# First loads in another order, and the queries' block diagonals loaded by their non-zero quarters

## The chip, the cores and the metric

The kernel runs on one core of a Trainium2 chip. A core has five engines that follow their own instruction streams and meet at semaphores: TensorE (PE; its weight load is PEld), VectorE (DVE), ScalarE (ACT), GpSimd (POOL) and SyncE (SP), which here issues all DMAs. Sixteen DMA engines move the data between the memory of the chip (HBM) and the core's own. The metric is the device time of one execution in microseconds (us); the profile is of another execution, taken by the hardware profiler.

## The reference

Inputs are q, k and v of 2 batches, 8 heads, 768 positions and 64 values per head. Each query attends to the positions less than 16 away, and to 24 summaries, one for each block of 32 positions. Two feed-forward layers follow.

```python
k_sum = k.reshape(B, H, nb, block, D).max(axis=3)
v_sum = v.reshape(B, H, nb, block, D).mean(axis=3)
scores_l = where(abs(i - j) < 16, scale * q @ k.T, -1e9)
scores_s = scale * q @ k_sum.T + log(32)
a = softmax(concatenate([scores_l, scores_s]))
x = a @ concatenate([v, v_sum])             # 1536 tokens x 512
h = x @ w_in                                # 512 x 1024, float64 weights
h = h * softmax(h); h = layer_norm(h) * g_ln
x = h @ w_out                               # 1024 x 512
out = elu(x @ w_in2) @ w_out2               # 512 x 2048, 2048 x 512
```

## The kernel before

**Attention.** The 1536 tokens are cut into 24 tiles of 64 queries (n = 0 to 23, twelve of each batch). For tile n, `attn_s(n)` multiplies the queries with a window of 96 keys and the 24 block maxima (four matmuls of 128x128 by 128x120, two heads each; 120 = 96 + 24), adds a mask and makes the softmax on VectorE, ScalarE and GpSimd. `attn_p(n)` transposes the result on TensorE, and `attn_x(j)` multiplies tiles 2j and 2j+1 with their values and splits the product into a high and a low part, `xT[j]`. To hold two heads in one matmul, the queries come as block diagonals: `qd[n]` is 128 partitions x 4 head pairs x 128, where partitions 0 to 63 have values in the first 64 columns of each pair alone, and partitions 64 to 127 in the last 64. The host writes the zeros. `load_q(n)` (L192) loads this block whole, 256 KB in rows of 2 KB, into one of four rotating buffers `q_bd`.

`load_k(b)` loads the keys of batch b in four DMAs of 400 KB, `sum_k(b)` takes the block maxima on VectorE. `sum_v(b)` (L181) loads the values of batch b in six DMAs of 256 KB and makes the block means with six products on TensorE (twelve matmul records), which use the constant `avg`. `load_v(n)` loads the 96 values' rows of tile n (192 KB) into one of four buffers `vws`. From tile 12 on `load_kw(n)` loads the window of keys of a tile (192 KB, as 512 pieces of 384 bytes); before, GpSimd copies it from the keys.

**Weights.** `w_in` is float64. It comes in eight pieces of 512 KB (n = 0, 1 and k = 0 to 3), each into one of six places `early`, and is converted by ScalarE, GpSimd and VectorE into two float32 parts (`convert`, L141). Before the change `load_w_in` (L154) issues the load and the conversion together, and `more()` (L443) takes the next of the eight. `w_out` follows in eight pieces (`load_w_out`, one in each of the ticks 2 to 9).

**Order.** After a warm-up of 32 matmuls on a tile of zeros (L463 to L467) comes a first part written out by hand (L471 to L499), then a loop over 24 ticks (L515). In tick t the attention runs ahead: `attn_s(t + 6)`, `attn_x` of tiles up to t + 3, `attn_p(t + 4)`, beside `mm_in(j, n)`, twelve matmuls of the first feed-forward layer. Tick 0 holds `sum_v(1)`, tick 1 begins with `load_k(1)`. Without a load in the text before it, `attn_s(n)` loads its own queries. The SP queue is in manual order: SP issues the DMAs as the program names them, and when one has to wait, those behind it wait too. The other engines' orders come from a planner that simulates a timeline. `v_sb` and the keys share two buffers (tag "k"), so that `load_k(1)` must wait until the products of `sum_v(1)` have read theirs.

Of the kernel before, what the change touches and what calls it, by code (L numbers as in the profile page):

```python
# [22 lines left out]
TQ = 64  # L23
# [14 lines left out]
NKW = 4  # L38
NV = 4
NCOPY = 12  # L40
NG = 4


# [10 lines left out]
def tile_kernel(ctx: ExitStack, tc: tile.TileContext, qd, kT, v, w_in, w_out, g_ln, w_in2, w_out2,  # L54
# [39 lines left out]
    kws = [p_at.tile([128, NP, KW], F32, name=f"kw{i}", bufs=1) for i in range(NKW)]  # L94
    vws = [p_at.tile([128, DM], F32, name=f"vw{i}", bufs=1) for i in range(NV)]
    avg = p_at.tile([128, 128 + NB], F32, name="avg", bufs=1)
    nc.gpsimd.memset(negh, -0.5)
    nc.gpsimd.memset(guard, 1e-12)

# [16 lines left out]
    def load_words(bits, src):  # L116
        nc.sync.dma_start(bits, src if len(src.shape) == 3 else src.rearrange("p (k f) -> p k f", k=KD))
# [33 lines left out]

    early = stage[0] + stage[1] + stage[2]

    def load_w_in(n, k):  # L154
        cs = slice(n * 512, (n + 1) * 512)
        convert(early[(n * KD + k) % 6], w_in[k * 128:(k + 1) * 128, cs].bitcast(I32),
                w_in_hl[0][:, k, cs], w_in_hl[1][:, k, cs])

    def load_w_out(k):
        load_words(early[k % 6], w_out[k * 128:(k + 1) * 128, :].bitcast(I32))  # L160
# [7 lines left out]
    def load_k(b):  # L168
        k_sb[b] = p_k.tile([128, NP, S + 2 * PAD], F32, tag="k", name="k_sb", bufs=2)
        for p in range(NP):  # L170
            nc.sync.dma_start(k_sb[b][:, p, :], kT[b, p])
# [7 lines left out]


    def sum_v(b):  # L181
        pst = psb.tile([128, DM], F32, tag="b", name="vs_ps")
        v_sb = p_k.tile([128, NP, S + 2 * PAD], F32, tag="k", name="v_sb", bufs=2).rearrange("p a s -> p (a s)")
        for i in range(S // 128):
            vt = v_sb[:, i * DM:(i + 1) * DM]
            nc.sync.dma_start(vt, v[b, PAD + i * 128:PAD + (i + 1) * 128, :])
            c0 = NB - i * 4
            nc.tensor.matmul(pst, lhsT=avg[:, c0:c0 + 128], rhs=vt, start=i == 0, stop=i == S // 128 - 1)
        vsum[b] = p_at.tile([128, DM], F32, tag="vsum", name="vsum", bufs=1)
        nc.scalar.activation(vsum[b][WIN:KW, :], pst[WIN:KW, :], AF.Copy)  # L190

    def load_q(n):  # L192
        q_bd[n] = p_at.tile([128, NP, 2 * TQ], F32, tag="q", name="q_bd", bufs=4)
        nc.sync.dma_start(q_bd[n], qd[n])

    def load_v(n):
        b, t = divmod(n, NT)
        nc.sync.dma_start(vws[n % NV][0:WIN, :], v[b, t * TQ:t * TQ + WIN, :])
# [237 lines left out]
        yf["B22"] = form("y1", b22)  # L436


    conv = [lambda n=n, k=k: load_w_in(n, k) for n in range(2) for k in range(KD)]
    words = [lambda k=k: load_w_out(k) for k in range(KF1)]  # L440
    parts = [lambda k=k: convert_w_out(k) for k in range(KF1)]

    def more(n=1):  # L443
        for _ in range(n):
            if conv:
                conv.pop(0)()

    def mm_in(j, n):
        for k in range(KD):
# [18 lines left out]

    loads = tc.manual_schedule(engines={mybir.EngineType.SP})
    loads.__enter__()  # L470
    load_k(0)  # L471
    load_q(1)
    load_v(0)
    nc.sync.dma_start(mask, mask_d)
    sum_k(0)
    nc.sync.dma_start(ident, ident_d)
    load_q(0)
    more()
    nc.sync.dma_start(avg, avg_d)
    attn_s(0)  # L480
    more()
    attn_s(1)
    sum_v(0)
    more(2)
    attn_p(0)
    attn_p(1)
    attn_s(2)
    load_v(1)
    attn_x(0)
    nc.sync.dma_start(gT, g_ln)  # L490
    attn_s(3)
    load_v(2)
    attn_p(2)
    attn_s(5)
    more(3)
    attn_p(3)
    attn_s(4)
    load_v(3)
    more()  # L499

# [12 lines left out]
    for t, (j, n) in enumerate(ticks):  # L515
        s_n, p_n, x_n = t + LEAD, t + LEAD - 2, t + LEAD - 3
        if t == 0:
            sum_v(1)
        elif t == 1:
            load_k(1)  # L520
        elif t == 3:
            sum_k(1)
        if t % 2:
            for u in (x_n, x_n + 1):
                if u < NU:
                    load_v(u)
        if s_n < NU:
            for u in (s_n + 1, s_n):
                if u < NU and u not in q_bd:
                    load_q(u)  # L530
            load_kw(s_n + 1)
            attn_s(s_n)
        if x_n < NU and x_n % 2:
            attn_x(x_n // 2)
        mm_in(j, n)
        if p_n < NU:
            attn_p(p_n)
        for f, *args in after[t]:
            f(*args)
        for _ in range(fetches.get(t, 0)):  # L540
            words.pop(0)()
        for _ in range(converts.get(t, 0)):
            parts.pop(0)()
        if t == min(late) - 1:
            fetch()
        if t == 14:
            spare[:] = stage[2]
        more_w(late.get(t, 0))
        if x_n == NU - 1:
            p_at.release()  # L550
            p_w3 = ctx.enter_context(tc.tile_pool(name="p_w3", bufs=1, side="left", reuse_waits="tile"))
            for f in (3, 4):
                w3t[f] = p_w3.tile([128, 2048], F32, tag=f"f{f}", name="w3f")
            w3e[0] = p_w3.tile([128, 2, 3, 2, 128], F32R, name="w3e")
            last_t = p_w3.tile([128, 2, KF1, TB], F32R, tag="last", name="lnT")
            lnT_last = [last_t[:, c] for c in range(2)]
# [229 lines left out]
```

## Time and profile before

| what | us |
|---|---|
| median of 3 runs (lowest to highest) | 479.52 (479.25 to 479.68) |
| profiled execution, its own time | 480.95 |
| its span, first to last instruction | 479.2 |
| TensorE busy | 464.0 |
| VectorE, ScalarE, GpSimd busy | 298.6, 286.9, 122.3 |
| DMA queue of the kernel, as a share of 16 engines | 52.1% |

The profiled execution lies 1.4 us above the median, and 1.75 us of it lie outside the span. Busy time of TensorE is the union of modelled instruction times: it holds the warm-up's matmuls too, and a busy stretch can hold small holes. Times in the rows count from the start of the span.

### The profile page before, as it was taken

How to read it: one execution, taken by the hardware profiler on the slowest of the kernel's cores; microseconds unless marked ns; L12 is line 12 of the kernel's file. 1: busy time of each engine (PE TensorE's matmuls, PEld its weight loads, DVE VectorE, ACT ScalarE, POOL GpSimd, SP SyncE). 2: the span in 40 equal slices, each digit the busy share in tenths (PEclk: the TensorE clock that was granted, in tenths of full speed). 3: DMA queues.
4: the chain of work that ended last, by engine and by line, in shares of the span. 5: the costliest groups of instructions: out<-in, count | busy, mean ns of one | idle time of the engine just before them, and what ended most of it. 6: DMA issues, size and time to landing. Idle time of an engine off the chain costs nothing.

```text
span 479.2 us, 7413 instructions
## 1 busy us (share of the span) xinstructions
PE 464.0 (97%) x2600; PEld 390.1 (81%) x2600; DVE 298.6 (62%) x664; ACT 286.9 (60%) x647; POOL 122.3 (26%) x213
## 2 busy tenths in 40 slices
PE   7789999899999999999999999999999999999996
PEld 3456788789988989999888888888888888888885
DVE  3786779885568529786998893367665565450000
ACT  1795697986568428475957673567667666560001
POOL 2795276755443512332222200000000000000000
PEclk9999999999999999999999999999999999999999
DMA  8996995462280543388879614442212222377112
GB/s 284 353 365 185 297 299 174 127 193 77 84 256 19 166 133 130 118 291 315 244 273 385 213 54 136 172 175 60 72 51 83 88 60 73 133 297 274 44 44 88
DMA packets 40116, 82.46 MB, mean 172 GB/s; under 512 B 9616, under 2 KB 18448, under 8 KB 40080
## 3 DMA queue, kind: packets, MB, share of 16 engines
q1 hardware_dynamic: 40080, 82.00, 52.1%
q8 instruction: 20, 0.33, 0.3%
q14 instruction: 16, 0.13, 0.1%
HBM read 70.46 MB, written 11.53 MB: 171 GB/s over the span
## 4 chain that ended last, share of the span: by engine, by line
PE 86%; DMA 8%; DVE 3%; ACT 1%; SPq 1%; issue 0%
PE o_ps L110 9%; PE o_ps L108 9%; PE o_ps L109 9%; PE h L110 7%; PE h L108 7%; PE h L109 7%; PE c L110 5%; PE c L108 5%; PE c L109 5%; DMA q_bd<-in_qd 5%; PE y_ps L108 5%; PE y_ps L110 5%; PE y_ps L109 5%; PE s_ps L218 3%; PE t_ps L299 2%; DMA vw<-in_v 2%
## 5 line engine op out<-in xcount | busy, mean ns | idle before, releaser
L129 POOL TENSOR_SCALAR conv<-conv 128x512 f32<-128x512 f32 x48 | 37.6, 785 | 81.2 <-ACT conv L126 79.6
L232 POOL TENSOR_SCALAR sm<-sm,st 128x120 f32<-128x120 f32 x96 | 43.8, 472 | 30.7 <-DVE st L230 14.3
L108 PE MATMUL o_ps<-w4r,g_hl 128*128 128x512 f32 x128 | 49.8, 389 | 0.0
L109 PE MATMUL o_ps<-w4r,g_hl 128*128 128x512 f32 x128 | 49.8, 389 | 0.0
L110 PE MATMUL o_ps<-w4r,g_hl 128*128 128x512 f32 x128 | 46.7, 389 | 0.0
L108 PE MATMUL y_ps<-lnT,w_out 128*128 128x384 f32 x128 | 43.6, 341 | 0.8 <-ACT y L316 0.8
L227 ACT ACTIVATE sm<-sm,st 128x120 f32<-128x120 f32 x96 | 37.0, 390 | 10.7 <-DVE st L224 10.7
L109 PE MATMUL y_ps<-lnT,w_out 128*128 128x384 f32 x128 | 43.2, 337 | 0.0
L110 PE MATMUL y_ps<-lnT,w_out 128*128 128x384 f32 x128 | 42.9, 336 | 0.0
L108 PE MATMUL h<-w_in,xT 128*128 128x512 f32 x96 | 39.3, 411 | 0.8 <-ACT xT L138 0.8
L110 PE MATMUL h<-w_in,xT 128*128 128x512 f32 x96 | 38.5, 401 | 0.8 <-DVE xT L105 0.8
L109 PE MATMUL h<-w_in,xT 128*128 128x512 f32 x96 | 38.4, 400 | 0.0
L224 DVE CUSTOM_DVE_ANT_0 sm<-s_ps,mask 128x120 f32<-128x120 f32 x96 | 21.6, 277 | 14.6 <-PE s_ps L218 14.2
L593 ACT ACTIVATE y<-y 128x512 f32<-128x512 f32 x48 | 30.0, 628 | 0.7
L621 DVE COPY y<-o_ps 128x512 f32<-128x512 f32 x5 | 3.5, 690 | 42.9 <-PE o_ps L110 42.9
L623 ACT ACTIVATE y<-o_ps 128x512 f32<-128x512 f32 x6 | 3.6, 600 | 43.9 <-PE o_ps L110 43.9
L105 DVE TENSOR_TENSOR g_hl<-y,g_hl 128x512 fp32r<-128x512 f32 x32 | 22.4, 701 | 11.3 <-ACT g_hl L138 11.2
L218 PE MATMUL s_ps<-kw,q_bd 128*128 128x120 f32 x192 | 25.9, 278 | 3.6 <-DMA q_bd<-in_qd 3.1
L218 PEld LDWEIGHTS s_ps<-kw,q_bd 128*128 128x128 f32 x192 | 23.9, 191 | 6.5 <-POOL kw L101 1.9
L109 PEld LDWEIGHTS o_ps<-w4r,g_hl 128*128 128x128 f32 x128 | 24.1, 188 | 5.1
L126 ACT ACTIVATE conv<-y 128x512 f32<-128x512 f32 x30 | 20.2, 676 | 13.3 <-DMA y<-in_w_in 11.3
L110 PEld LDWEIGHTS o_ps<-w4r,g_hl 128*128 128x128 f32 x128 | 24.0, 188 | 5.0
(148 smaller groups left out, 1239.9 us busy)
## 6 DMA issues: line engine op xcount, KB each, us to landing
w4r<-w4d SPq DMA_DIRECT2D x38, 512.0 KB, 3.4
y<-in_w_in SPq DMA_DIRECT2D x16, 512.0 KB, 5.9
w4d<-w3f SPq DMA_DIRECT2D x16, 512.0 KB, 3.4
y<-in_w_out SPq DMA_DIRECT2D x14, 512.0 KB, 7.0
q_bd<-in_qd SPq DMA_DIRECT2D x24, 256.0 KB, 7.0
bits<-in_w_out SPq DMA_DIRECT2D x10, 512.0 KB, 5.0
w4l<-w4d SPq DMA_DIRECT2D x10, 512.0 KB, 4.6
vw<-in_v SPq DMA_DIRECT2D x24, 192.0 KB, 6.5
```

Of the source, the lines that this page charges most:

```text
L105: nc.vector.tensor_tensor(out_, x, hi.bitcast(F32), op=ALU.subtract)
L108: nc.tensor.matmul(ps, lhsT=l[0][ls], rhs=r[0][rs], start=first, stop=False, skip_group_check=parts)
L109: nc.tensor.matmul(ps, lhsT=l[0][ls], rhs=r[1][rs], start=False, stop=False, skip_group_check=parts)
L110: nc.tensor.matmul(ps, lhsT=l[1][ls], rhs=r[0][rs], start=False, stop=last, skip_group_check=parts)
L126: first = nc.scalar.activation(x, high.bitcast(F32), AF.Prelu, scale=TO_F32, alpha=SIGN_TO_28)
L129: nc.gpsimd.tensor_scalar(x, x, MOST, LEAST, op0=ALU.min, op1=ALU.max)
L218: nc.tensor.matmul(sps[:, p, 0:KW], lhsT=q_bd[n][:, p, :], rhs=kw[:, p, :], start=True, stop=True)
L224: nc.vector.tensor_tensor_reduce(sm[:, p, :], sps[:, p, 0:KW], mask[:, mi, :], -scale, 3.0e38, op0=ALU.add, op1=ALU.min, accum_out=nm[:, p ...
L227: nc.scalar.activation(sm[:, p, :], sm[:, p, :], AF.Exp, bias=nm[:, p:p + 1], scale=-1.0, accum_out=ss[:, p:p + 1])
L232: nc.gpsimd.tensor_scalar(sm[:, p, :], sm[:, p, :], ri[:, p:p + 1], 1.0, op0=ALU.mult, op1=ALU.mult)
L299: nc.tensor.transpose(tp[:, i, :], es[j][:, k * 128:(k + 1) * 128], ident)
L593: nc.scalar.activation(m, m, AF.Exp, scale=-1.0)
```

## The change

The four buffers for the queries become fixed tiles (`qs`, in turn n % 4). VectorE writes the zeros of each once, with eight memsets of 64 partitions x 256 at the very beginning of the program. `load_q` loads the two non-zero quarters alone: two DMAs of 64 partitions x 4 pairs x 64 values, 64 KB each in pieces of 256 bytes. The mask comes in three DMAs of 60 KB. Loads and conversions of `w_in`, and loads and products of `sum_v`, are split, and the order on the SP queue is rewritten; `load_k(1)` goes behind the loads of tick 1. The number of matmuls and conversions stays.

```diff
+    qs = [p_at.tile([128, NP, 2 * TQ], F32, name=f"q_bd{i}", bufs=1) for i in range(NQ)]
+    for t in qs:
+        for hh in range(2):
+            nc.vector.memset(t[hh * D:(hh + 1) * D, :, (1 - hh) * TQ:(2 - hh) * TQ], 0.0)
...
     def load_q(n):
-        q_bd[n] = p_at.tile([128, NP, 2 * TQ], F32, tag="q", name="q_bd", bufs=4)
-        nc.sync.dma_start(q_bd[n], qd[n])
+        q_bd[n] = qs[n % NQ]
+        for hh in range(2):
+            ds, cs = slice(hh * D, (hh + 1) * D), slice(hh * TQ, (hh + 1) * TQ)
+            nc.sync.dma_start(q_bd[n][ds, :, cs], qd[n, ds, :, cs])
...
     load_k(0)
+    load_q(0)
+    load_mask(1)
     load_q(1)
+    load_mask(0)
+    nc.sync.dma_start(ident, ident_d)
+    words_w_in(0)
     load_v(0)
-    nc.sync.dma_start(mask, mask_d)
+    words_w_in(1)
+    nc.sync.dma_start(avg, avg_d)
+    means = sum_v(0)
+    load_v(1)
+    words_w_in(2)
+    words_w_in(3)
+    load_q(2)
+    load_q(3)
+    load_v(2)
+    nc.sync.dma_start(gT, g_ln)
+    words_w_in(4)
+    load_v(3)
+    words_w_in(5)
     sum_k(0)
-    nc.sync.dma_start(ident, ident_d)
-    load_q(0)
-    more()
-    nc.sync.dma_start(avg, avg_d)
+    convert_w_in(0)
     attn_s(0)
-    more()
+    convert_w_in(1)
     attn_s(1)
-    sum_v(0)
-    more(2)
+    means()
+    convert_w_in(2)
+    convert_w_in(3)
     attn_p(0)
     attn_p(1)
     attn_s(2)
-    load_v(1)
     attn_x(0)
-    nc.sync.dma_start(gT, g_ln)
     attn_s(3)
-    load_v(2)
     attn_p(2)
+    words_w_in(6)
     attn_s(5)
-    more(3)
+    convert_w_in(4)
+    convert_w_in(5)
+    convert_w_in(6)
     attn_p(3)
+    words_w_in(7)
     attn_s(4)
-    load_v(3)
-    more()
+    convert_w_in(7)
+    load_mask(2)
...
         if t == 0:
-            sum_v(1)
-        elif t == 1:
-            load_k(1)
+            sum_v(1)()
...
             load_kw(s_n + 1)
+            if t == 1:
+                load_k(1)
             attn_s(s_n)
```

## Rows read from the trace of the kernel before

**Rows 1.** the page: span, and busy time of each engine
```profile
span 479.2 us, 7413 instructions
...
PE 464.0 (97%) x2600; PEld 390.1 (81%) x2600; DVE 298.6 (62%) x664; ACT 286.9 (60%) x647; POOL 122.3 (26%) x213
```

**Rows 2.** windows: busy us of PE, PEld, DVE, ACT, POOL, clock, DMA share, GB/s
```profile
10.00:20.00 10.00, 7.13 (x31) 4.39 (x32) 5.64 (x25) 6.04 (x21) 7.47 (x16) 1.00 1.04 399
...
30.00:40.00 10.00, 8.75 (x39) 5.40 (x38) 8.12 (x30) 7.15 (x23) 9.67 (x16) 1.00 0.67 244
40.00:50.00 10.00, 9.42 (x80) 7.85 (x79) 6.72 (x25) 6.18 (x21) 3.06 (x8) 1.00 0.88 257
50.00:60.00 10.00, 9.55 (x112) 7.82 (x110) 7.37 (x30) 6.56 (x23) 3.58 (x11) 1.00 1.05 301
...
80.00:90.00 10.00, 8.79 (x84) 7.49 (x82) 9.31 (x34) 8.27 (x23) 5.08 (x9) 1.00 0.39 114
```

**Rows 3.** the chain in order of time: start, length (us), what
```profile
2.57 6.94 DMA q_bd<-in_qd
9.53 5.22 DMA v_sb<-in_v
14.77 7.47 DMA q_bd<-in_qd
...
42.53 8.54 DMA vw<-in_v
51.13 8.85 DMA q_bd<-in_qd
```

**Rows 4.** timeline of TensorE: start, us, instruction, idle before and releaser
```profile
1.17 8.82 PE L467 MATMUL busy<-ln 128*128 128x512 bf16 x32 [1.17 <-DVE ln L464]
11.40 2.02 PE L218 MATMUL s_ps<-kw,q_bd 128*128 128x120 f32 x16 [1.41 <-DMA q_bd<-in_qd]
...
31.49 1.05 PE L218 MATMUL s_ps<-kw,q_bd 128*128 128x120 f32 x8
...
34.12 1.96 PE L188 MATMUL vs_ps<-v_sb,avg 128*128 128x512 f32 x4 [1.25 <-DVE st L230]
...
46.51 0.50 PE L110 MATMUL h<-w_in,xT 128*128 128x512 f32 x1 [0.58 <-DVE xT L105]
...
51.86 1.12 PE L218 MATMUL s_ps<-kw,q_bd 128*128 128x120 f32 x8 [0.26 <-DMA q_bd<-in_qd]
52.91 1.15 PE L254 MATMUL x_ps<-pT,vw 120*64 120x64 f32 x32
...
60.12 1.12 PE L218 MATMUL s_ps<-kw,q_bd 128*128 128x120 f32 x8 [0.23 <-DMA q_bd<-in_qd]
```

**Rows 5.** timeline of the SP queue: start and length of each issue
```profile
8.60 0.33 SPq L117 DMA_DIRECT2D y<-in_w_in  x1
...
24.86 6.20 SPq L186 DMA_DIRECT2D v_sb<-in_v  x6
...
40.23 1.75 SPq L171 DMA_DIRECT2D k_sb<-in_kT  x4
```

**Rows 6.** DMA issues begun at 23.29, 24.86, 92.31: KB, us to landing
```profile
q_bd<-in_qd SPq DMA_DIRECT2D x1, 256.0 KB, 7.4
...
v_sb<-in_v SPq DMA_DIRECT2D x1, 256.0 KB, 9.1
...
y<-in_w_in SPq DMA_DIRECT2D x1, 512.0 KB, 3.8
```

**Rows 7.** DMA packets of the stretches 56 to 59 and 60 to 63 us
```profile
DMA packets 412, 1.00 MB, mean 334 GB/s; under 512 B 52, under 2 KB 52, under 8 KB 412
...
DMA packets 760, 0.95 MB, mean 316 GB/s; under 512 B 510, under 2 KB 510, under 8 KB 758
```

**Rows 8.** timeline of VectorE, first 4 us
```profile
0.84 0.27 DVE L464 MEMSET ln<- 128x256 f32 x1 [0.84 <-PEq L778]
3.80 0.95 DVE L176 TENSOR_REDUCE kw<-k_sb 128x24 f32<-128x768 f32 x1 [2.69 <-DMA k_sb<-in_kT]
```

More of the change, by code (lines that the diff above doesn't have):

```diff
@@ L40 @@
 NCOPY = 12
+NQ = 4
 NG = 4
@@ L152, in tile_kernel, with words_w_in, convert_w_in @@
     early = stage[0] + stage[1] + stage[2]
-    def load_w_in(n, k):
+    def words_w_in(i):
+        n, k = divmod(i, KD)
+        load_words(early[i % 6], w_in[k * 128:(k + 1) * 128, n * 512:(n + 1) * 512].bitcast(I32))
+    def convert_w_in(i):
+        n, k = divmod(i, KD)
         cs = slice(n * 512, (n + 1) * 512)
-        convert(early[(n * KD + k) % 6], w_in[k * 128:(k + 1) * 128, cs].bitcast(I32),
-                w_in_hl[0][:, k, cs], w_in_hl[1][:, k, cs])
+        convert(early[i % 6], None, w_in_hl[0][:, k, cs], w_in_hl[1][:, k, cs])
     def load_w_out(k):
@@ L181, in sum_v, with products @@
     def sum_v(b):
-        pst = psb.tile([128, DM], F32, tag="b", name="vs_ps")
         v_sb = p_k.tile([128, NP, S + 2 * PAD], F32, tag="k", name="v_sb", bufs=2).rearrange("p a s -> p (a s)")
-        for i in range(S // 128):
-            vt = v_sb[:, i * DM:(i + 1) * DM]
+        vts = [v_sb[:, i * DM:(i + 1) * DM] for i in range(S // 128)]
+        for i, vt in enumerate(vts):
             nc.sync.dma_start(vt, v[b, PAD + i * 128:PAD + (i + 1) * 128, :])
[L187 to L190, printed above, removed]
+        def products():
+            pst = psb.tile([128, DM], F32, tag="b", name="vs_ps")
+            for i, vt in enumerate(vts):
+                c0 = NB - i * 4
+                nc.tensor.matmul(pst, lhsT=avg[:, c0:c0 + 128], rhs=vt, start=i == 0, stop=i == S // 128 - 1)
+            vsum[b] = p_at.tile([128, DM], F32, tag="vsum", name="vsum", bufs=1)
+            nc.scalar.activation(vsum[b][WIN:KW, :], pst[WIN:KW, :], AF.Copy)
+        return products
     def load_q(n):
-        q_bd[n] = p_at.tile([128, NP, 2 * TQ], F32, tag="q", name="q_bd", bufs=4)
-        nc.sync.dma_start(q_bd[n], qd[n])
+        q_bd[n] = qs[n % NQ]
+        for hh in range(2):
+            ds, cs = slice(hh * D, (hh + 1) * D), slice(hh * TQ, (hh + 1) * TQ)
+            nc.sync.dma_start(q_bd[n][ds, :, cs], qd[n, ds, :, cs])
     def load_v(n):
@@ L436, in forms_late @@
         yf["B22"] = form("y1", b22)
-    conv = [lambda n=n, k=k: load_w_in(n, k) for n in range(2) for k in range(KD)]
     words = [lambda k=k: load_w_out(k) for k in range(KF1)]
     parts = [lambda k=k: convert_w_out(k) for k in range(KF1)]
[L443 to L446, printed above, removed]
     def mm_in(j, n):
@@ L470, in tile_kernel, with load_mask @@
     loads.__enter__()
+    def load_mask(m):
+        nc.sync.dma_start(mask[:, m], mask_d[:, m])
     load_k(0)
+    load_q(0)
+    load_mask(1)
     load_q(1)
+    load_mask(0)
+    nc.sync.dma_start(ident, ident_d)
+    words_w_in(0)
     load_v(0)
-    nc.sync.dma_start(mask, mask_d)
+    words_w_in(1)
[11 more added lines that the diff above has]
+    words_w_in(5)
     sum_k(0)
-    nc.sync.dma_start(ident, ident_d)
-    load_q(0)
-    more()
-    nc.sync.dma_start(avg, avg_d)
+    convert_w_in(0)
     attn_s(0)
-    more()
+    convert_w_in(1)
     attn_s(1)
-    sum_v(0)
-    more(2)
+    means()
+    convert_w_in(2)
+    convert_w_in(3)
     attn_p(0)
```

## The prediction

> **What bounds the kernel now.** I read the page first, for the size of what can be had. TensorE is busy 464.0 of 479.2 us [rows 1]; the change leaves each matmul in place, so it can only win idle time: 15.2 us, 1.17 of it before the first matmul [rows 4]. The windows show where the rest lies: among them 2.87 us from 10 to 20, 1.25 from 30 to 40, 0.58 and 0.45 from 40 to 60, and 1.21 from 80 to 90 [rows 2]. Then the chain of waits says what sets the pace. Up to 22 us it is a pure chain of loads: a load of queries issued at 2.57 lands 6.94 later, at 9.51; a load of v_sb follows at 9.53 and lands at 14.75; queries follow at 14.77 and land at 22.24 [rows 3]. Counted in the text of the kernel these are the 5th, the 13th and the 21st DMA of SP. So the reader is to see a rule of this kernel's queue: a DMA goes out when the one eight places ahead has landed, however many bytes either has. At 42.53 and 51.13 the chain is on loads again (values, queries).
>
> For what TensorE waits on there I read its timeline and, beside it, the issues. Its first s_ps waits 1.41 us for queries. At 34.12 the profile puts a gap of 1.25 us down to VectorE; but the line is the first product of `sum_v(1)`, whose data was issued at 24.86 and took 9.1 us, to 33.98 [rows 4, 5, 6]. VectorE had long been done; the load was late. At 51.86 and 60.12 short gaps end with queries, 0.49 us together [rows 4].
>
> **The packets.** A load of queries was 128 pieces of 2 KB, and becomes two DMAs of 256 pieces of 256 bytes: half the bytes, four times the pieces. The trace before has no piece of 256 bytes. The nearest are those of 384 bytes of the key windows. In two full stretches of 3 us, one has 412 packets and 1.00 MB, the other 760 and 0.95 MB, with 458 more below 512 bytes [rows 7]. These 458 carry 0.176 MB; the other 0.774 MB would take 2.32 us at the pace of the first stretch; 0.68 us x 16 engines / 458 leaves 23.8 ns a piece. A 2 KB piece at 334 GB/s on 16 engines takes 98 ns. The line through both gives 18.1 ns for 256 bytes; in proportion to the bytes it would be 15.9, and it can hardly be above 23.8. A load of queries then takes 512 x 18.1 / 16 = 0.58 us (0.51 to 0.76), where 0.262 MB took 0.78 us at 334 GB/s and 0.66 at the 399 GB/s of 10 to 20 us [rows 2]. I take a saving of 0.15 us a load, with -0.10 to 0.27 as bounds.
>
> Against the change stands a rule of the Trainium skill ("DMA: Bandwidth & Descriptors", Specifications): full rate needs pieces of at least 512 bytes, since smaller ones are read, modified and written. The trace agrees only in part: 384 bytes in 23.8 ns are 16 bytes a nanosecond, 2 KB in 98 are 21, a fifth less and no doubling. By the rule as a doubling of the 18.1 ns the sum would be that of the last rival below.
>
> **The first loads.** The eight memsets write 256 elements per partition each; the one before took 0.27 us for as many [rows 8], so 2.16 us in all. VectorE is idle until the first keys, 2.69 us [rows 8], so they hide there. But they stand ahead of the memset that the warm-up waits for. If VectorE keeps that order, the 8.82 us of warm-up begin at 3.3 and end at 12.15, where the first s_ps began at 11.40 [rows 4]: it loses 0.75 us, or nothing if the planner swaps them. I take nothing, because the chain at 22 us hangs on queries that land, not on what tile 0 does; without that cover the 0.75 would be paid.
>
> The queries of tile 0 come ahead of those of tile 1, so the 1.41 us are not waited for the load any more; I count no gain, since the chain of loads decides later. There the count of eight bites. In the new order four halves of queries, two pieces of mask and `ident` stand behind the keys, and the first piece of `w_in` is the 12th DMA. The 12th went out at 8.60 before [rows 5] and will again, since the keys ahead of it are the same. Then only some 0.45 MB are in flight. A `w_in` load with nothing ahead of it took 3.8 us to land [rows 6], so this one lands at 12.4 at best. Behind it come 192 KB of values and the second piece: 0.49 + 1.31 us at 399 GB/s, so 14.2. Before, the second piece was itself the 12th, just ahead of the v_sb load that landed at 14.75 [rows 3]: 14.75 - 0.66 = 14.1. The new order thus starts the long stream some 0.1 us later, in spite of fewer bytes. From there to the first load of `sum_v(1)` both orders hold the same loads, but `avg` (0.2) now falls behind and a third of the mask (0.15) is added, and four loads of queries save 0.15 each. Sum: 0.1 + 0.2 + 0.15 - 0.6 = -0.15, so that load lands at 33.8 and not 33.98. The gap at 34.12 shrinks by 0.15; with the best packets by 0.6, and with the worst it grows by 0.85.
>
> **The blocked queue.** Keys of batch 1 went out at 40.23 [rows 5], the moment the last product of `sum_v(1)` had freed their buffer; values 4 and 5 and queries 8, which need no such buffer, stood behind them on SP. They landed from 50 us on: the chain has the second load of values at 51.07 [rows 3], and s_ps of tile 8 (51.86) and x_ps of tiles 4 and 5 (52.91) follow at once [rows 4]. In the new order they stand ahead and go out from about 35 us. What is late next is the keys themselves, which still go at about 40, and `w_out`, which gains those 0.64 MB: 2.1 us at 301 GB/s [rows 2]. So TensorE gets x_ps of tiles 4 and 5, and with it fresh matmuls of the first layer, some microseconds earlier. What it can win is its idle time from 40 to 60, 1.03 us [rows 2]; 0.49 of it is put down to queries. I take 0.9, most of it, because the 0.58 at 46.51 [rows 4] too lies where TensorE had no other product ready, and an earlier x_ps is one. Bounds 0 and 1.03. Two DMAs for one on SP cost another issue of 0.33 us [rows 5] and a place of eight; from 40 on SP mostly waits for landings, so neither is on the path.
>
> **Later.** From 80 to 90 TensorE idles 1.21 us while VectorE is busy 9.31 of 10 [rows 2]. Earlier `w_out` words let conversions move into 50 to 60, where ScalarE has 3.4 us free. I take 0.25 of it; the bounds are a loss of as much idle time again and the whole.
>
> Sum: -0.15 - 0.9 - 0.25 = -1.3 us, on the profiled execution (480.95) as on the median: 479.52 - 1.3 = 478.2. Best packets, the whole 1.03 and the whole 1.21 would give -2.8, 476.7.
>
> **Rivals.**
> (a) The relief is given back. VectorE and ScalarE set the pace from 77 to 91 us; if TensorE comes there earlier and only waits longer, or the 0.75 of the warm-up is paid, 0 to 0.9 is left: 478.7 to 479.8. For it: VectorE's 9.31 of 10. Against: its work hangs on TensorE's, so it moves ahead too.
> (b) Slower. The queries of tile 4 now stand behind two pieces of `w_in` and just ahead of a third of the mask and v_sb: 33.8 - 0.66 - 0.15 = 33.0, where they landed at 30.7 (issued at 23.29, 7.4) [rows 6]. Their s_ps ran at 31.49 [rows 4]; it would run at 33.1, 1.6 us late, and with it a softmax on GpSimd, which has 0.33 of 10 us free there [rows 2]. If TensorE's order keeps this s_ps ahead of other ready work, and GpSimd can't catch up, this costs 1.6 less the 0.15: 481.0. It decides as soon as the queries land later than about 31.4. Against: before 40 us TensorE still has the products of `sum_v(1)` to fill in.
> (c) The small packets cost double: 36.2 ns, 1.16 us a load, 0.44 us more than the mean of before, eight times on the stream: +3.5, 483.0. It turns from gain to loss at 21 to 24.5 ns a piece. The rule above is for it, the 384-byte rows are against.
>
> **How the numbers follow.** Relief as summed 0.50, (a) 0.30, (b) 0.14, (c) 0.06. A change of 0.2% (1.0 us) is about what can be told from none: faster 0.50, same 0.30, slower 0.20. The likeliest, 478.2, is the prediction; its own range is 476.7 to 478.6. The range reaches over (a) to (b): 476.6 to 481.0, leaving out (c) and the worst of (b).
>
> **What the new profile would show.** Query loads of two DMAs with 512 packets below 512 bytes and full stretches no slower than 0.58 us each; the memset of the warm-up at 0.84 or at 3.0; first product of `sum_v(1)` near 33.8; values 4 and 5 issued before the keys of batch 1 and x_ps of tiles 4 and 5 before 50 us; idle time from 40 to 60 below 0.3. The prediction is wrong if the planner lays TensorE's order differently, if s_ps of tile 4 is what everything waits for near 33, or if the idle time turns up again from 80 to 95.

## The result, and the profile after

The changed kernel took 482.67 us (median of 22 executions, 479.72 to 485.56) against 479.53 for the kernel before beside it (22, 478.43 to 481.68). The ratio is 1.0065, with a 95% interval of 1.0052 to 1.0078: slower by 3.1 us, where 478.2 and a gain of 1.3 had been forecast. The range ended at 481.0 and did not hold it.

One thing has to be known before the profile is read. The profiled execution of the changed kernel took 479.72, its fastest of 22. Each execution comes with its mean granted TensorE clock; this one alone had 1.000. Seven had 0.996 and a mean of 482.17, six 0.993 and 482.88, eight 0.988 to 0.991 and 483.89. The 22 executions of the kernel before that ran beside the first experiments lie at 0.998 to 1.000. So the rows below show what the new order does when the clock holds; a second profile, in the experiments, shows it when the clock falls. By its span, 477.9 against 479.2 us, this one execution has the forecast gain of 1.3 us; but it is one of 22, the profile of the kernel before was itself 1.4 us above its median, and the parts of the sum did not come as forecast (below), so the agreement is luck.

The page (span, busy time of each engine, DMA packets) and, under it, the windows (busy us of PE, PEld, DVE, ACT, POOL, then clock, DMA share, GB/s):

```profile
span 477.9 us, 7458 instructions
...
PE 463.7 (97%) x2600; PEld 390.1 (82%) x2600; DVE 299.7 (63%) x672; ACT 286.9 (60%) x647; POOL 118.0 (25%) x213
...
DMA packets 50005, 79.33 MB, mean 166 GB/s; under 512 B 22704, under 2 KB 31408, under 8 KB 49968
```

```profile
10.00:20.00 10.00, 8.59 (x40) 4.93 (x38) 4.61 (x24) 5.14 (x20) 4.15 (x10) 1.00 0.99 324
20.00:30.00 10.00, 7.20 (x62) 4.74 (x60) 5.31 (x25) 7.74 (x24) 9.44 (x19) 1.00 1.07 341
30.00:40.00 10.00, 10.00 (x49) 6.68 (x48) 8.69 (x31) 7.09 (x24) 8.85 (x15) 1.00 0.96 285
40.00:50.00 10.00, 10.00 (x86) 8.28 (x85) 9.25 (x31) 6.79 (x22) 4.78 (x10) 1.00 0.82 264
50.00:60.00 10.00, 10.00 (x84) 8.52 (x83) 8.53 (x36) 8.96 (x32) 6.79 (x19) 1.00 1.05 292
...
80.00:90.00 10.00, 8.72 (x84) 7.28 (x83) 8.91 (x40) 9.18 (x27) 5.98 (x11) 1.00 0.31 86
```

From 30 to 60 us TensorE has no idle time left; before it idled 2.28 us there [rows 2]. That is the forecast gain, and more. The 1.28 us from 80 to 90 stay (1.21 before), so the 0.25 forecast of it did not come. What was lost lies ahead of 30 us: there TensorE idles 8.3 us (4.07 before its first matmul, 1.41 and 2.80 in the next windows), where it idled 6.3 in the kernel before (1.17 and 2.87 [rows 2, 4], and 2.29 by this row of its windows):

```profile
20.00:30.00 10.00, 7.71 (x69) 5.82 (x68) 8.10 (x28) 8.29 (x26) 9.02 (x16) 1.00 1.06 321
```

The timeline of TensorE (start, length, instruction, idle time before it and its releaser), and under it three rows of the kernel before:

```profile
4.07 9.01 PE L476 MATMUL busy<-ln 128*128 128x512 bf16 x32 [4.07 <-DVE ln L473]
12.92 1.94 PE L233 MATMUL s_ps<-kw,q_bd 128*128 128x120 f32 x16
16.27 5.39 PE L200 MATMUL vs_ps<-v_sb,avg 128*128 128x512 f32 x12 [1.41 <-DMA v_sb<-in_v]
...
24.05 1.12 PE L233 MATMUL s_ps<-kw,q_bd 128*128 128x120 f32 x8 [0.68 <-DMA q_bd<-in_qd]
...
29.55 0.50 PE L113 MATMUL h<-w_in,xT 128*128 128x512 f32 x1 [2.06 <-ACT xT L143]
...
34.19 1.05 PE L233 MATMUL s_ps<-kw,q_bd 128*128 128x120 f32 x8
```

```profile
14.89 1.95 PE L188 MATMUL vs_ps<-v_sb,avg 128*128 128x512 f32 x4 [1.47 <-DMA v_sb<-in_v]
...
22.38 1.12 PE L218 MATMUL s_ps<-kw,q_bd 128*128 128x120 f32 x8 [1.22 <-DMA q_bd<-in_qd]
...
26.70 0.50 PE L108 MATMUL h<-w_in,xT 128*128 128x512 f32 x1 [0.83 <-ACT xT L138]
```

The warm-up begins 2.90 us later than before and so does not end before 13 us; the first s_ps comes at 12.92 and not 11.40 [rows 4]. The first product of the values comes at 16.27 and not 14.89, the s_ps of tile 2 at 24.05 and not 22.38. The first product of the first layer (`h`) comes at 29.55; before, it came at 26.70. The s_ps of tile 4 runs at 34.19, late as rival (b) had it, and no hole stands ahead of it.

The SP queue (start and length of each issue), and the DMA issues of four stretches (KB each, median us to landing), those that begin at 8.81, at 26.64, at 28.62 and at 36.75:

```profile
8.81 0.33 SPq L122 DMA_DIRECT2D y<-in_w_in  x1
...
28.62 5.43 SPq L194 DMA_DIRECT2D v_sb<-in_v  x6
34.15 2.50 SPq L209 DMA_DIRECT2D q_bd<-in_qd  x4
36.75 1.01 SPq L213 DMA_DIRECT2D vw<-in_v  x2
37.89 1.47 SPq L209 DMA_DIRECT2D q_bd<-in_qd  x2
41.47 1.78 SPq L180 DMA_DIRECT2D k_sb<-in_kT  x4
```

```profile
y<-in_w_in SPq DMA_DIRECT2D x1, 512.0 KB, 4.8
...
q_bd<-in_qd SPq DMA_DIRECT2D x2, 64.0 KB, 6.7
...
v_sb<-in_v SPq DMA_DIRECT2D x1, 256.0 KB, 5.8
...
vw<-in_v SPq DMA_DIRECT2D x1, 192.0 KB, 3.5
```

Values 4 and 5 and queries 8 now go out ahead of the keys of batch 1, which stand at 41.47 (40.23 before [rows 5]); values 4 landed 3.5 us after 36.75, at 40.25, where values 4 and 5 had landed from 50 us on. The first load of `sum_v(1)` landed at 34.4 (28.62 + 5.8; forecast 33.8). But the first piece of `w_in`, the 12th DMA, landed 4.8 us after 8.81, at 13.6, against 12.4 "at best" in the prediction. Ahead of it the stream of loads runs dry. This is the window from 8 to 10 us, first of the changed kernel, then of the new order with one DMA a load (an experiment below); the last two numbers are the share of the time in which the DMA engines are busy, and GB/s:

```profile
8.00:10.00 2.00, 2.00 (x11) 0.92 (x10) 1.33 (x2) 0.00 (x0) 1.04 (x3) 1.00 0.41 88
```

```profile
8.00:10.00 2.00, 2.00 (x11) 0.94 (x10) 0.95 (x1) 0.00 (x0) 1.83 (x4) 1.00 1.09 382
```

The timeline of VectorE up to its first softmax, and the first softmax of the kernel before:

```profile
0.83 2.81 DVE L101 MEMSET q_bd<- 64x256 f32 x8 [0.83 <-PEq L806]
3.75 0.27 DVE L473 MEMSET ln<- 128x256 f32 x1
...
15.01 0.43 DVE L135 TENSOR_SCALAR conv<-conv 128x512 int32<-128x512 int32 x1 [5.24 <-POOL conv L134]
...
16.08 0.28 DVE L239 CUSTOM_DVE_ANT_0 sm<-s_ps,mask 128x120 f32<-128x120 f32 x1
```

```profile
12.56 0.28 DVE L224 CUSTOM_DVE_ANT_0 sm<-s_ps,mask 128x120 f32<-128x120 f32 x1 [3.01 <-PE s_ps L218]
```

A memset of 64 x 256 takes 0.35 us (2.81 / 8), more than the 0.27 of 128 x 256 [rows 8]. And the first softmax stands behind the conversion of the late piece of `w_in`: 16.08, where it came at 12.56 before, though its s_ps began at 12.92.

### The profile page after: what moved, and what is told of

The parts are those of the page before. It is cut to its first block, busy times and chain, and to the rows that moved or that the text cites. A ratio compares the mean times of both kernels' runs of the same rounds, so it can differ in the third digit from the quotient of the medians.

```text
span 477.9 us, 7458 instructions
## 1 busy us (share of the span) xinstructions
PE 463.7 (97%) x2600; PEld 390.1 (82%) x2600; DVE 299.7 (63%) x672; ACT 286.9 (60%) x647; POOL 118.0 (25%) x213
## 4 chain that ended last, share of the span: by engine, by line
PE 92%; DMA 4%; ACT 2%; SPq 1%; issue 0%; DVE 0%
PE o_ps L115 9%; PE o_ps L114 9%; PE o_ps L113 9%; PE h L113 8%; PE h L115 8%; PE h L114 8%; PE c L115 5%; PE c L113 5%; PE c L114 5%; PE y_ps L113 5%; PE y_ps L115 5%; PE y_ps L114 5%; PE s_ps L233 4%; PE x_ps L269 2%; PE p_ps L252 2%; PE t_ps L314 2%
## 5 line engine op out<-in xcount | busy, mean ns | idle before, releaser
L134 POOL TENSOR_SCALAR conv<-conv 128x512 f32<-128x512 f32 x48 | 35.1, 733 | 79.1 <-ACT conv L131 77.5
L247 POOL TENSOR_SCALAR sm<-sm,st 128x120 f32<-128x120 f32 x96 | 42.6, 461 | 31.5 <-DVE st L245 19.2
L114 PEld LDWEIGHTS o_ps<-w4r,g_hl 128*128 128x128 f32 x128 | 24.1, 188 | 5.1
L115 PEld LDWEIGHTS o_ps<-w4r,g_hl 128*128 128x128 f32 x128 | 24.0, 188 | 5.0
L113 PEld LDWEIGHTS o_ps<-w4r,g_hl 128*128 128x128 f32 x128 | 24.0, 188 | 5.0
L135 DVE TENSOR_SCALAR conv<-conv 128x512 int32<-128x512 int32 x48 | 22.0, 460 | 8.1 <-POOL conv L134 8.1
```

The source lines that it names most:

```text
L113: nc.tensor.matmul(ps, lhsT=l[0][ls], rhs=r[0][rs], start=first, stop=False, skip_group_check=parts)
L114: nc.tensor.matmul(ps, lhsT=l[0][ls], rhs=r[1][rs], start=False, stop=False, skip_group_check=parts)
L115: nc.tensor.matmul(ps, lhsT=l[1][ls], rhs=r[0][rs], start=False, stop=last, skip_group_check=parts)
L134: nc.gpsimd.tensor_scalar(x, x, MOST, LEAST, op0=ALU.min, op1=ALU.max)
L135: nc.vector.tensor_scalar(a, a, 3, None, op0=ALU.logical_shift_left)
L247: nc.gpsimd.tensor_scalar(sm[:, p, :], sm[:, p, :], ri[:, p:p + 1], 1.0, op0=ALU.mult, op1=ALU.mult)
```

## The experiments

Each is timed against the kernel before on the chip that it ran on; the median of that was 479.6 to 480.0 each time. After the median stand the lowest and highest time and the number of executions; ratios are to the kernel before, with their 95% interval. "Clock" is the mean over a kernel's executions.

### The change taken apart

The same kernel once more, for a second profile (no edit).

> The changed kernel as it is, one more look, to see in which stretch TensorE's granted clock falls. In the profile at hand the clock is 1.00 from 8 us on and the time is 479.7; 21 other executions had a mean clock of 0.988 to 0.996 and took 481 to 486. Theory A (clock): a stretch of some 4 to 12 us at 1.2 GHz lies between 10 and 32 us, where TensorE idles most, and the rest is as in the profile at hand. Theory B (order and queue): the loss would lie in longer waits for loads, with the clock no different where TensorE works.

Measured: 481.61, clock 0.996. Windows of this profile, and under them the same stretch of the first profile:

```profile
26.00:29.00 3.00, 3.00 (x25) 2.67 (x25) 2.12 (x10) 1.66 (x9) 1.54 (x3) 0.50 0.96 292
```

```profile
26.00:29.00 3.00, 1.48 (x24) 1.23 (x23) 2.84 (x17) 3.00 (x14) 2.84 (x5) 1.00 1.03 348
```

The granted clock is 0.50 here, the lower of its two levels (1.2 GHz), and 25 matmuls keep TensorE busy for all 3.00 us, where 24 took 1.48 (not the same ones in each: the second profile is 1.25 us behind). TensorE's timeline of the second profile shows what came before it:

```profile
25.30 1.52 PE L233 MATMUL s_ps<-kw,q_bd 128*128 128x120 f32 x8 [2.08 <-DMA q_bd<-in_qd]
...
31.47 0.50 PE L113 MATMUL h<-w_in,xT 128*128 128x512 f32 x1 [1.21 <-ACT xT L143]
```

A wait of 2.08 us for queries, then the low clock. The first `h` comes 1.92 us later than in the first profile (31.47 - 29.55), and the span is 1.9 longer (479.8 against 477.9): what is lost at the start is not won back. Of the 1.92, the s_ps ahead is 1.25 late (25.30 - 24.05), from a later landing, before the clock fell; 0.67 come after it, under the low clock. The Trainium skill ("TensorE: Matmul & The Clock Gate", HAM oscillation) tells of a kernel whose waits for DMA make the clock fall again and again; this trace shows one such fall, after a wait of 2 us.

The new order with whole query blocks, without memsets:

```diff
-    qs = [...]; for t in qs: ... nc.vector.memset(...)
 def load_q(n):
-        q_bd[n] = qs[n % NQ]
-        for hh in range(2): ... nc.sync.dma_start(q_bd[n][ds, :, cs], qd[n, ds, :, cs])
+        q_bd[n] = p_at.tile([128, NP, 2 * TQ], F32, tag="q", name="q_bd", bufs=4)
+        nc.sync.dma_start(q_bd[n], qd[n])
```

> The new order of loads with whole blocks of queries in one DMA each, and so without the eight memsets. Theory A1 (the memsets start the warm-up 2.9 us late and the first stretch then has holes in which the clock falls): warm-up at 1.2 us again, clock near 1.00, 476 to 479. Theory A2 (the new order makes the holes: the first piece of w_in lands late and VectorE waits for it in its order): still 481 to 484. Theory C (small packets): 1 us or more below the changed kernel.

Measured: 480.75 (479.53 to 482.38, 12), 1.0015 [1.0001, 1.0030], clock 0.992. Its SP queue, the issue of the first `w_in` piece, and TensorE's holes:

```profile
5.71 0.43 SPq L118 DMA_DIRECT2D y<-in_w_in  x1
```

```profile
y<-in_w_in SPq DMA_DIRECT2D x1, 512.0 KB, 6.3
```

```profile
14.97 1.10 PE L196 MATMUL vs_ps<-v_sb,avg 128*128 128x512 f32 x2 [2.03 <-DMA v_sb<-in_v]
...
23.25 1.20 PE L227 MATMUL s_ps<-kw,q_bd 128*128 128x120 f32 x8 [2.01 <-DMA q_bd<-in_qd]
...
28.95 0.50 PE L109 MATMUL h<-w_in,xT 128*128 128x512 f32 x1 [0.78 <-ACT xT L139]
```

With one DMA a load, this piece is the 10th and goes out at 5.71, 3.10 us earlier than with two; it lands at 12.0 and not 13.6, and the first v_sb product starts at 14.97 and not 16.27. The time lies between the ranges of theories A1 and A2, and where theory C has it; the halves below decide on C. Of the 0.65%, 0.5 go with the quarters and memsets. But the order alone does not win either, although it holds the relief of the blocked queue: its s_ps of tile 2 is 0.87 us and its first `h` 2.25 us later than before (23.25 against 22.38, 28.95 against 26.70).

The old order with quarters and memsets:

```diff
 def load_q(n):
-        q_bd[n] = p_at.tile([128, NP, 2 * TQ], F32, tag="q", name="q_bd", bufs=4)
-        nc.sync.dma_start(q_bd[n], qd[n])
+        q_bd[n] = qs[n % NQ]   # with the eight memsets of the change
+        for hh in range(2): ... nc.sync.dma_start(q_bd[n][ds, :, cs], qd[n, ds, :, cs])
```

> The old order of loads, with the queries by quarters and the eight memsets. Theory A1: warm-up at 4.1 us and a clock below 1.00, 480.5 to 484. Theory A2: as the kernel before or a little faster, 478 to 480, as half the bytes of the queries are gone. Theory C: slower than before by 0.5 to 3 us, with the clock at 1.00.

Measured: 488.86 (488.36 to 489.7, 4), 1.0182 [1.0165, 1.0198], clock 0.993. Quarters and memsets in the old order cost 8.7 us, more than any of the theories had. SP's timeline and TensorE's:

```profile
14.51 2.47 SPq L122 DMA_DIRECT2D y<-in_w_in  x2
...
26.31 1.55 SPq L122 DMA_DIRECT2D y<-in_w_in  x3
```

```profile
33.21 0.50 PE L113 MATMUL h<-w_in,xT 128*128 128x512 f32 x1 [0.70 <-ACT xT L143]
```

The next `w_in` piece goes out 9.3 us after the issues of a pair that end at 16.98; nine DMAs stand between, seven of them of 64 KB or less. Before, six stood there, and it took 5.0 us. From 25 to 26.3 us the DMA share is 0.12 (33 GB/s), where it was 1.03 (413 GB/s) in the kernel before: the stream has run dry. The first `h` falls to 33.21.

### Two DMAs, or small pieces?

Whole blocks, loaded as two DMAs of 64 partitions with rows of 2 KB, in the old order and in the new one; no memsets:

```diff
-        nc.sync.dma_start(q_bd[n], qd[n])
+        for hh in range(2):
+            ds = slice(hh * D, (hh + 1) * D)
+            nc.sync.dma_start(q_bd[n][ds], qd[n, ds])
```

> The kernel before with the queries in two DMAs of 64 partitions, whole rows, no memsets. Theory D (places of eight): most of the 9 us that quarters cost in the old order come back, 485 to 489, with pauses of the stream between 20 and 32 us where several of the eight places hold halves of queries behind one piece of w_in. Rival C (small pieces or memsets): 479.5 to 481.

> The new order with the queries in two DMAs of 64 partitions each, whole rows of 2 KB with their zeros, no memsets: as many DMAs as the changed kernel, as many bytes as before, no piece of 256 bytes. Theory D (two DMAs take two of the eight places, so fewer bytes are in flight when the first piece of w_in goes out at 8.8): the first load of v_sb lands at 15.5 to 16.2, as with quarters, and the time is 481 to 484. Rival C (small pieces or memsets are what costs): that load lands near 14.8 and the time is 480 to 481, as with whole blocks.

Measured: old order 487.63 (484.65 to 488.8, 6), 1.0161 [1.0137, 1.0186]; new order 484.63 (484.09 to 485.26, 5), 1.0091 [1.0079, 1.0104]. In the old order TensorE stands at the first product of `sum_v(1)` (before: 34.12 [rows 4]):

```profile
37.50 3.43 PE L188 MATMUL vs_ps<-v_sb,avg 128*128 128x512 f32 x4 [1.39 <-DMA v_sb<-in_v]
```

Without one small piece the cost is nearly that of the quarters (1.6 against 1.8%). So it lies in loading a block by two DMAs of 64 partitions, not in the size of the pieces. Which part of that costs is not shown: each load takes two of the eight places, and each DMA reaches half of the partitions; no run has two DMAs of 128 partitions. In the new order the stream runs dry as in the changed kernel (DMA share 0.28 from 10 to 11 us), and the first v_sb product comes at 17.71, later than theory D had it. With halves in the old order it does not: from 20 to 30 us the DMA share stays at 1.01 (1.06 before), but at 277 GB/s where the kernel before moved 321. "DMA: Bandwidth & Descriptors" of the Trainium skill (Rules for kernel authors) says of two transfers to disjoint partition halves that they serialize, and to use one of 128 partitions. That one is better these runs bear out; that the halves serialize no run here shows.

The quarters of the first four tiles on ScalarE's queue:

```diff
-            nc.sync.dma_start(q_bd[n][ds, :, cs], qd[n, ds, :, cs])
+            (nc.scalar if n < NQ else nc.sync).dma_start(q_bd[n][ds, :, cs], qd[n, ds, :, cs])
```

> The changed kernel with the eight DMAs for the queries of tiles 0 to 3 issued by ScalarE on its own queue, so that they take none of SP's eight places; same bytes, same pieces. Theory D (places): the first piece of w_in goes out before 6 us and lands before 12.6, the first load of v_sb lands before 15.4, and the time is 480 to 481.5, near the new order with whole blocks (480.75) or below. Rival (pieces of 256 bytes and memsets are what costs beside the order): 482 to 484, as the changed kernel.

Measured: 489.58 (485.13 to 490.75, 6), 1.0176 [1.0142, 1.0211], far above both ranges. The timeline of ScalarE, and the packets of its queue in the first 14 us (count, MB, share of 16 engines):

```profile
0.72 10.30 ACTq L209 DMA_DIRECT2D q_bd<-in_qd  x8
```

```profile
q10 hardware_dynamic: 1858, 0.45, 14.6%
```

ScalarE stood 10.3 us at eight issues, which it would need for its own work, and the first `w_in` piece, only the 8th DMA on SP, still waited until 9.57. The places are shared by both queues, so a second queue frees none. The trace says why: the landings of all 235 DMAs of this run, of both queues, are counted on eight semaphores, 29 or 30 on each, and so it is with the 209 of the kernel before. The eight places are thus the eight semaphores of this program, and no run shows a limit of the chip at eight. On the price of two DMAs the run decides nothing. But it prices the small pieces, since this queue carries hardly anything else: 14.6% of 14 us on 16 engines, over 1858 packets, is 17.6 ns each.

Whole blocks for tiles 0 to 3, without memsets, quarters from tile 4 on (whose zeros the whole blocks have brought):

```diff
+        if n < NQ:
+            nc.sync.dma_start(q_bd[n], qd[n])
+            return
         for hh in range(2): ...
```

> The changed kernel with whole blocks, one DMA each, for tiles 0 to 3; they bring the zeros, so the memsets are gone; quarters from tile 4 on. Theory D (two DMAs a load cost in the first part): 479.8 to 481.3, as the new order with whole blocks, ratio to before 1.000 to 1.003. Rival C2 (the quarters of tiles 4 to 8, on the stream up to 40 us, cost as much as the first): 481.5 to 483.

Measured: 480.27 (478.08 to 480.88, 12), 1.0006 [0.9992, 1.0019], clock 0.995. That gives back 0.6% of the 0.65 with four DMAs fewer and no memsets, at the start only. In its profile the first v_sb product comes at 14.82 and the s_ps of tile 2 at 23.11, near those of the new order with whole blocks (14.97 and 23.25). The two executions with a clock of at least 0.998 took 478.08 and 478.17, the ten others a mean of 480.33.

### The late warm-up

The eight memsets behind the warm-up's start:

```diff
     nc.tensor.matmul(busy[:, 0:512], lhsT=zero[:, 0:128], rhs=zero, start=True, stop=True)
+    for t in qs: ... nc.vector.memset(...)   # moved from the head of the kernel
```

> The changed kernel with the eight memsets behind the warm-up's memset. Theory A1: warm-up at 1.2 us, first s_ps near 11.5, clock near 1.00, 476 to 478.5, faster than both. Theory A2: warm-up at 1.2 us, but the holes between 13 and 30 us stay or grow, the clock falls as often, 481 to 484. Theory C: no better than 481, with the clock at 1.00.

Measured: 483.04 (480.7 to 485.18, 11), 1.0059 [1.0042, 1.0076], clock 0.991. TensorE:

```profile
1.17 8.43 PE L473 MATMUL busy<-ln 128*128 128x512 bf16 x32 [1.17 <-DVE ln L470]
...
17.49 2.05 PE L197 MATMUL vs_ps<-v_sb,avg 128*128 128x512 f32 x2 [4.44 <-DMA v_sb<-in_v]
```

The warm-up starts early again, and nothing is won: it then ends long before the values are there, and a hole of 4.44 us follows. I had thought the late warm-up the main cause; this run speaks against it. It is no clean test, as its first `w_in` load goes out at 9.50 and not 8.81, and its values land 1.2 us later than in the changed kernel (17.49 against 16.27).

The reverse: the new order with whole blocks, and eight memsets of the same size into memory not yet in use ahead of the warm-up:

```diff
+    for i in range(4):
+        for hh in range(2):
+            nc.vector.memset(ln_t[hh * D:(hh + 1) * D, i, 0:256], 0.0)
```

> The new order with whole blocks, and eight memsets of 64 partitions x 256 into memory that is free then, ahead of the warm-up's memset as in the changed kernel. It isolates the memsets. Theory D: the DMAs and not the memsets cost, 480 to 481.5, though the warm-up begins at 4.1. Rival C3 (the late warm-up costs the 2 us between whole blocks and quarters): 482 to 483.5.

Measured: 481.50 (479.77 to 482.63, 11), 1.0031 [1.0018, 1.0043], against 1.0015 [1.0001, 1.0030] without them. The memsets may cost 0.16%; the intervals overlap.

### The holes and the clock

22 matmuls of zeros into the holes: 8 behind s_ps of tile 1, 6 behind p_ps of tile 1, 8 behind the first x_ps; once in the changed kernel, once in the new order with whole blocks:

```diff
+    def filler(last, count):
+        with tc.issue_after(last.ins):
+            for _ in range(count):
+                nc.tensor.matmul(busy[:, 0:512], lhsT=zero[:, 0:128], rhs=zero, start=True, stop=True)
```

> The changed kernel with 22 more matmuls on zeros (the warm-up's form), put where TensorE waits: 8 behind s_ps of tile 1, 6 behind the transposes of tile 1, 8 behind the first x_ps. They add 4.7 us of TensorE time and no result. Theory A (the loss is the clock that falls in the holes of the first 32 us): the clock stays at 1.00 in nearly all executions, median 479.0 to 480.5, that is 2 to 3.5 us faster than the changed kernel, and the spread between executions falls below 1.5 us. Rival (waits for loads and places in the queue are the loss, the clock only goes with them): no faster, 482 to 485, since work is added.

> The new order with whole blocks of queries, with the same 22 matmuls in the holes. Theory A: clock at 1.00, median 477.5 to 479, faster than the kernel before by 0.2% or more. Rival: no faster than the same order without them, 480.5 to 482.

Measured: 484.65 (484.08 to 486.15, 5), 1.0096 [1.0080, 1.0111], clock 0.995; and 481.82 (480.78 to 483.29, 10), 1.0037 [1.0024, 1.0050], clock 0.999. In the second the clock holds, as expected (0.992 without them), but the kernel is 0.2% slower than without the fillers. They are some 5 us of TensorE's time (8 take 1.89), and not all of it falls into holes. In the first the first `h` moves to 31.90. Filling is no cure, and no clean measure of what the clock costs. Theory A missed both times.

A warm-up of 8 matmuls in place of 32 in the kernel before:

```diff
-    for i in range(32):
+    for i in range(8):
         nc.tensor.matmul(busy ...
```

> The kernel before with a warm-up of 8 matmuls, not 32. Loads and order stay; TensorE then waits from about 4.6 to 11.4 us. Theory A (a clock that falls in the first part is paid in time): the clock is at 1.2 GHz for longer in the first 30 us, mean 0.985 to 0.994, and the time is 481 to 483, 1.5 to 3 us slower at unchanged landings. Rival (the clock of the first part hides behind the loads): 479.5 to 480.2 in spite of the clock.

Measured: 480.27 (478.66 to 481.99, 12), 1.0002 [0.9987, 1.0017], clock 0.994. The six executions at 0.989 took a mean of 480.65, the three at 1.000 479.13, three at 0.999 480.11. The low clock goes with 1.5 us within this kernel, and its median stays where it was.

### The order within the start

The first `w_in` piece right behind the queries of tile 0; the queries of tiles 2 and 3 ahead of values 1 and `w_in` pieces 2 and 3, in the changed kernel and with whole blocks:

```diff
     load_k(0)
     load_q(0)
+    words_w_in(0)            # first variant; taken out further down
...
     means = sum_v(0)
+    load_q(2); load_q(3)     # second and third variant; taken out further down
     load_v(1)
```

> The changed kernel with the first piece of w_in moved up by six places, right behind the queries of tile 0, so that 0.5 MB more are in flight when the keys have landed. Theory D (thin queue): no pause of the stream near 11 us, that piece lands near 10.7 and no longer at 13.6, VectorE starts the first softmax near 13.5 and not 16.1, the first load of v_sb lands near 15.0; 479 to 481.5, with fewer falls of the clock. Rival A (memsets and late warm-up): as the changed kernel, 482 to 484.

> The changed kernel with the queries of tiles 2 and 3 ahead of the values of tile 1 and of two pieces of w_in. Theory F (in the new order the hole ahead of s_ps of tile 2, where TensorE waits for its queries at 23 to 25 us, is what the clock falls over): the hole shrinks below 0.7 us, the clock falls in fewer executions (mean 0.996 or more), 480 to 481.5. Rival D (the hole is only moved: another load of the same stream is late by as much, here the second and third pieces of w_in): a hole as long elsewhere before 32 us, clock near 0.993 as in the changed kernel, 482 to 483.5.

> The same move in the new order with whole blocks of queries. Theory F: clock 0.996 or more on the mean, 478.5 to 480, faster than before if the relief of the later part is kept. Rival D: 480.5 to 481.5, clock near 0.992.

Measured: 483.43 (482.15 to 484.79, 6), 1.0068 [1.0051, 1.0084]; 485.32 (482.81 to 487.25, 6), 1.0117 [1.0092, 1.0142]; 482.11 (481.02 to 483.26, 6), 1.0048 [1.0033, 1.0063]. None helps, and the last two are slower than either theory had them. The first brings its piece at 10.93 and the first softmax to 14.29, and from 8 to 10 us the stream no longer runs dry (DMA share 0.97, 275 GB/s); yet the s_ps of tile 2 comes at 24.60, `h` at 30.23, and the time stays. The second brings `h` to 27.63, but opens other holes (1.00 at 31.20, 1.00 at 32.94, 1.25 at 60.23, 1.33 at 93.56) and takes 482.3 us of span in a profile at a clock of 0.999. So the clock is not the whole story, and the place of these queries is not what makes the new order late.

### The gain by itself

The kernel before with one step moved, the load of the keys of batch 1 behind the other loads of its step:

```diff
-        elif t == 1:
-            load_k(1)
...
             load_kw(s_n + 1)
+            if t == 1:
+                load_k(1)
             attn_s(s_n)
```

> The kernel before with one part of the change alone: the keys of batch 1 go behind the loads of tick 1. Theory E (the prediction's blocked queue): values 4 and 5 and queries 8 land before 45 and not from 50 on, the idle time from 40 to 60 falls from 1.0 to below 0.3 us, first part and clock as before (0.998 to 1.000): 478.6 to 479.3, 0.7 to 1.3 us faster than before. Rival (relief given back to VectorE and ScalarE from 80 to 95): 479.6 to 480.2, idle time from 80 to 95 larger by as much.

Measured: 478.66 (477.75 to 478.96, 8), 0.9976 [0.9967, 0.9986], clock 1.000 in seven of eight. SP's timeline and the windows:

```profile
33.17 0.96 SPq L198 DMA_DIRECT2D vw<-in_v  x2
34.51 0.35 SPq L194 DMA_DIRECT2D q_bd<-in_qd  x1
39.36 1.77 SPq L171 DMA_DIRECT2D k_sb<-in_kT  x4
```

```profile
40.00:50.00 10.00, 10.00 (x114) 8.65 (x114) 8.46 (x35) 6.68 (x26) 3.24 (x8) 1.00 0.96 305
50.00:60.00 10.00, 9.75 (x87) 8.57 (x86) 8.35 (x31) 9.13 (x32) 5.64 (x17) 1.00 1.07 325
...
80.00:90.00 10.00, 8.77 (x83) 7.60 (x82) 8.41 (x38) 10.00 (x31) 6.36 (x11) 1.00 0.26 78
```

Values 4 and 5 and queries 8 go out 5 us ahead of the keys, and the idle time from 40 to 60 falls from 1.03 [rows 2] to 0.25 us. From 80 to 90 it stays (1.23, before 1.21): the relief is neither given back there nor added to. This is the forecast relief, 1.1 us of it, without any of the rest. It has the lowest ratio of the study and beats both kernels.

The same with quarters from tile 8 on, no memsets:

```diff
+        if n < 2 * NQ:
+            nc.sync.dma_start(q_bd[n], qd[n])
+            return
         for hh in range(2): ... # quarters
```

> The kernel before with the keys of batch 1 moved behind the loads of tick 1, and with quarters for tiles 8 to 23 alone; tiles 0 to 7 come as whole blocks into the four fixed places, zeros included, so that no memset is needed. Theory D (the places cost where the stream from HBM sets the pace, that is up to 40 us): 478.2 to 479, no slower than with the moved keys alone (478.66). Rival C (two DMAs and small pieces cost anywhere): 480 to 483.

Measured: 479.22 (478.06 to 480.34, 12), 0.9983 [0.9970, 0.9997], just above the range of theory D. Later in the kernel the quarters neither cost nor win anything that can be told: the interval overlaps that of the whole blocks.

## Why the prediction was wrong

**The relief was right in its mechanism.** Forecast were -0.9 for the blocked queue; the moved keys alone give 0.9976, -1.1 us. Values and queries were issued and TensorE's idle time from 40 to 60 closed as written, by 0.78 us. The -0.25 for later did not come: from 80 to 90 TensorE idles as before (1.23 and 1.28 us, 1.21 before). That the two forecast terms together, -1.15, meet the -1.1 is luck.

**The step that failed** is the term of the first loads: that the new order "starts the long stream some 0.1 us later", and the -0.15 us made of it at the gap of 34.12. Set against the moved keys alone, the rest of the change cost 0.9% (1.0065 over 0.9976), some 4.3 us. The count of eight had been found, and the issue of the first `w_in` piece was forecast nearly right (8.60, measured 8.81). What was mis-sized is what follows from it. The piece was priced as if it would land in the 3.8 us of a load with nothing ahead [rows 6]; it took 4.8. The first v_sb product starts 1.38 us later than before (16.27 against 14.89), where 0.1 was forecast for the stream; with one DMA a load it starts 0.08 later (14.97). And the sum looked for the price at 34.12 alone, a gap that closed. It had no term for TensorE's waits ahead of 30 us, though 1.47 us for values and 1.22 for the queries of tile 2 stood there before. There the idle time grew by some 1.9 us, and the first `h` came 2.85 us later.

That of the second issue and the second place "neither is on the path" was said of the stretch from 40 us on, and there no cost can be told (0.9983 with quarters from tile 8 on). At the start the two DMAs do cost. With two DMAs a load, eight places hold 64 KB halves and other small loads, and the first 512 KB piece of `w_in` goes out 3.1 us later than with one (8.81 against 5.71). By the runs in which only this changes, two DMAs of 64 partitions for each whole block cost 1.6% in the old order and 0.8% in the new one (1.0091 against 1.0015). Which late load carries the loss is not shown: moving that piece of `w_in` up ended the dry stretch from 8 to 10 us and won nothing (1.0068).

**The packets were sized right.** Rival (c), 36 ns a piece, falls: the pieces of 256 bytes took 17.6 ns on ScalarE's queue, where the sum had 18.1. Halves with rows of 2 KB cost nearly as much as quarters in the old order, and more than the changed kernel in the new one.

**The memsets** were priced at nothing because "the chain at 22 us hangs on queries". They take 2.81 us and not 2.16, and hold the warm-up to 4.07 and not 3.3. Run by themselves they are 0.16% with overlapping intervals: a small term, and putting them behind the warm-up's start hardly helped (1.0059). The first s_ps at 12.92 is late by twice the 0.75 named.

**Rival (b)** had the queries of tile 4 right (landed from 33.3 on, forecast 33.0), but TensorE had first-layer matmuls to fill in, 10.00 of 10 us busy. The sign was that of this rival, and its mechanism was not the cause.

**The clock** was in no term of the sum. The start now has waits of 2 us, and in 21 of 22 executions the clock is granted below 0.997. Among these 21, time rises with the missing clock by 0.26 us for each 0.001 (a line through them); at the mean of 0.993 that would be 1.9 of the 3.1 us. The one execution at 1.000 even lies 1.4 us below that line, level with the kernel before. But late landings and a low clock come together, as in the second profile (1.25 us the one, 0.67 the other), so this is no price of the clock by itself.

By ratios the 0.65% come out so: keys of batch 1 later, -0.24 (measured by itself); the rest of the new first order, +0.39 (1.0015 over 0.9976); memsets, +0.16 (uncertain); two DMAs a load, with half the bytes, +0.34 (1.0065 over 1.0031). The last two together are tested directly for the first four tiles, by the run with whole blocks there: 1.0006, so 0.6 of the 0.65%.

**What stays open** is why the new first order costs 0.39%. Its profile shows two waits of 2 us and a first `h` 2.25 us late, and the re-ordering of it that was tried made it worse (1.0048). The planner orders the other engines' work anew in every variant (VectorE's first softmax moved by 3.5 us), so none of these runs changes a single wait. For the same reason the share of the clock isn't settled: whole blocks in the new order have a lower mean clock (0.992) than the changed kernel (0.993) and are 1.9 us faster, and with the fillers they are slow at 0.999. Nor is it separated what a place and what a load of half the partitions costs in the price of two DMAs.

## What to carry to other kernels

Where a program lets a fixed number of DMAs go at a time, count DMAs before bytes: here half the bytes in twice the DMAs left 88 GB/s from 8 to 10 us, where one DMA a load moved 382. Price a late load at every wait that follows it, and not only at one gap of the old profile. Try each part of a change by itself: here a single moved load won 0.24%, and the parts packed with it cost 0.9%. A profiled execution can be the best of many, as here; look at the clock of all executions before its span is believed.

## What was not expected of the hardware

- A piece of 256 bytes took 17.6 ns. In proportion to the bytes it would be 12.3 by the prediction's estimate of 98 ns for 2 KB: 1.4 times as long, and no doubling.
- What was not the hardware: the eight places are this program's eight semaphores, over SP's and ScalarE's queues together, and ScalarE stood 10.3 us at eight issues of 64 KB.
- After a wait of 2.08 us for a load the granted clock was 0.50 from 26 to 29 us. The mean clock was below 0.997 in 21 of 22 executions of the changed kernel and in one of eight of the best. Holding the clock with added matmuls cost more than it gave (1.0037 against 1.0015).
- A memset of 64 x 256 elements on VectorE took 0.35 us, one of 128 x 256 0.27.
